# Rearranging the first two chunks of a fused retention and feed-forward kernel: load order, rounding order, matmuls of the identity, relative decays and another tail

## Chip, cores, metric

The kernel runs on one core of one Trainium2 chip. The metric is the device time of one execution in microseconds (us). A ratio of two kernels is the mean time of one kernel's fast runs over that of the other's of the same rounds, so it is not quite the ratio of the medians that are quoted beside it. Profiles show single executions: the profiled one of the kernel before took 1091.1 us, so a difference of two traces can be off by one or two us.

## The reference

```python
B, H, S, D = 8, 8, 576, 64                      # q, k, v: float32
scores = q @ k.transpose(0, 1, 3, 2) / sqrt(D)
gamma = 1 - 2.0 ** (-5 - arange(H))
ret = scores * where(i >= j, gamma ** (i - j), 0)   # per head
x = (ret @ v).transpose(0, 2, 1, 3).reshape(4608, 512)
h = x @ w_in                                    # 512 x 2048
g = h * erf(softplus(h))
out = g @ w_out                                 # 2048 x 512
```

## The kernel before

The retention is computed in 40 pieces of at most 128 tokens (five a batch, the fifth of 64). Each piece has three stages: `transposes` (q and k through TensorE, later q through VectorE), `scores` (TensorE, then a masked copy to `sT` on VectorE) and `outputs` (sT times v, q times the running state, the new k^T v, and the scaled result into the chunk's tile `x`). 512 tokens make a chunk. For each of nine chunks and each of four groups of hidden columns, a block `First` makes seven products of a Strassen-like scheme with w_in, and a block `Second` seven with w_out. I call the products by their operand: A11 is the first of a `First`, A12 its second, T2 the third of a `Second`. The prediction also writes T7, S7 and O7 for the three stages of piece 7; where it says T2 of chunk 0, it means the product.

Weights are rounded on the chip before use. A group has four parts of w_in and four of w_out; a part takes ScalarE, VectorE and GpSimd in turn, and the generator yields between steps, so that the program can place them:

```python
def rounding():
    while words:
        while words[0][2] > most_g[0]:
            yield
        ...
        nc.scalar.activation(a_f, high_f, AF.Abs)
        nc.scalar.mul(out=r_f, in_=low, mul=2.0**-52)
        yield
        nc.vector.tensor_scalar(out=a_f, in0=a_f, ..., op0=ALU.max, op1=ALU.min)
        yield
        nc.vector.tensor_scalar(out=a, in0=a, ..., op0=ALU.logical_shift_left, op1=ALU.bitwise_and)
        yield
        nc.vector.scalar_tensor_tensor(out=a, in0=high, ..., in1=a, ...)
        yield
        nc.vector.tensor_scalar(out=high, in0=a, ..., op0=ALU.bitwise_and)
        nc.gpsimd.tensor_tensor(out=r_f, in0=high_f, in1=r_f, op=ALU.mult)
        nc.gpsimd.tensor_tensor(out=a_f, in0=a_f, in1=r_f, op=ALU.add)
        load_weights()
        yield
        if sums:                       # last part of a group: four sums on VectorE
            yield from sums(*(w[:, i] for i in range(7)))
```

Every engine and the DMA-issuing SyncE take their instructions in order:

```python
load(0, "qkv"); ...constants...; load(1, "qkv"); load(2)    # load(2): k and v only
for _ in range(3):
    load_weights()
...
while done[0] < stages_for(TCH):          # pieces 0 to 3
    attend(done[0] + 1)
    if done[0] >= 2:
        round_weights(2)
operands_x(0, 0)                          # chunk 0's operands, and their store to DRAM
run(firsts[0].first(), (0, 1), 2)         # products, stages and rounding steps in turn
run(firsts[0].middle(), (0, 1, 2), 2)
run(firsts[0].last(), (0, 1), 2)
firsts[0].erf()
...
```

`operands_x` ends with `nc.sync.dma_start(out=xd[c], in_=t)`: groups 1 to 3 read the chunk's operands back from DRAM. The pool of `x` tiles has two buffers, so chunk 2's tile takes chunk 0's buffer and must wait for that store. In the tail, the last chunk's `multiply` (two products h * erf on VectorE) follows `last()` of the block before.

## Time and profile before

| | before |
|---|---|
| median of three runs | 1088.3 us (1087.9 to 1090.1) |
| span of the trace | 1089.4 us |
| TensorE busy | 1051.2 us |
| TensorE idle in the first 123.3 us | 29.3 us |
| TensorE idle in the last 29.4 us | 9.0 us |

Four moments divide the execution: the start of A11 of chunk 0 (42.3 us), of A11 of chunk 1 (88.1), of T2 of chunk 0 (123.3), and the start of the last product that is made in the same stretch in both kernels (1056.8). The line below is the stretch between the last two in the kernel before: length, then busy us and number of instructions for PE, PEld, DVE, ACT, POOL, then granted clock, DMA share and GB/s.

```profile
123.34:1056.80 933.46, 933.46 (x5480) 805.80 (x5477) 539.62 (x905) 349.63 (x430) 82.65 (x71) 1.00 0.49 165
1056.80:1089.40 32.60, 23.65 (x105) 19.24 (x103) 14.01 (x20) 7.16 (x7) 0.00 (x0) 1.00 0.17 66
```

The first line is TensorE without a gap at full clock. The second is the tail, 32.60 us, in which it idles 9.

### The profile page before, as it was taken

The page shows a single profiled execution, that of the slowest core. Times are in us where ns is not written, and L with a number is a line of the kernel's source. Part 1 is how long each engine was busy: PE and PEld are TensorE (multiplying, and loading weights), DVE is VectorE, ACT ScalarE, POOL GpSimd, SP SyncE. Part 2 cuts the span into 40 slices and gives each one's busy share as a digit, 9 for nine tenths or more (in the row PEclk, how much of TensorE's full clock was granted, in tenths as well). Part 3 has the DMA queues.
Part 4 walks back from the last instruction along what each step waited for, and adds up shares of the span by engine and source line. Part 5 has one row for each costly group of instructions (what it writes and reads, how often), then busy time and mean ns, then how long its engine had stood idle before and what let it go on. Part 6 is the DMA issues. An engine that isn't in the chain of part 4 may idle for free.

```text
span 1089.4 us, 15783 instructions
## 1 busy us (share of the span) xinstructions
PE 1051.2 (96%) x6472; PEld 901.3 (83%) x6472; DVE 625.4 (57%) x1074; ACT 397.2 (36%) x501; POOL 124.7 (11%) x110
## 2 busy tenths in 40 slices
PE   4899899999999999999999999999999999999996
PEld 3677788888888888888888888888888888888885
DVE  3738677577667663455555545555655445445444
ACT  2224322414324244433334444333344433333340
POOL 3313221121121000010001100110010000000000
PEclk8989899999999999999999999999999999999999
DMA  9787584665753253355555533555544333444432
GB/s 199 174 187 170 119 223 135 143 191 123 173 165 76 110 193 107 145 184 189 202 201 205 185 149 145 184 193 199 204 187 146 145 145 145 174 181 191 178 116 78
DMA packets 170376, 178.60 MB, mean 164 GB/s; under 512 B 144448, under 2 KB 144448, under 8 KB 162240
## 3 DMA queue, kind: packets, MB, share of 16 engines
q1 hardware_dynamic: 170160, 177.23, 51.5%
q8 instruction: 51, 0.84, 0.3%
q10 hardware_dynamic: 144, 0.36, 0.1%
q14 instruction: 21, 0.17, 0.1%
HBM read 123.30 MB, written 54.26 MB: 163 GB/s over the span
## 4 chain that ended last, share of the span: by engine, by line
PE 92%; DVE 3%; SPq 2%; DMA 2%; POOL 0%; issue 0%; DVEq 0%; POOLq 0%
PE a L511 23%; PE a L432 23%; PE g L511 12%; PE g L432 11%; PE e L432 6%; PE e L511 6%; PE o L323 3%; PE s L311 3%; PE o L334 3%; SPq L115 2%; PE kv L346 2%; PE pt_k L296 1%; DMA raw_q<-in_q_dram 1%; DVE t L92 1%; DMA wraw<-in_moe_w_in_dram 1%
## 5 line engine op out<-in xcount | busy, mean ns | idle before, releaser
L432 PE MATMUL a<-x,wa 128*128 128x256 f32 x1152 | 276.1, 383 | 0.0
L432 PEld LDWEIGHTS a<-x,wa 128*128 128x128 f32 x1152 | 217.4, 191 | 30.6 <-issue 0.4
L511 PE MATMUL a<-wb,s 128*128 128x256 f32 x864 | 205.9, 381 | 2.3 <-DVE o L92 2.3
L511 PEld LDWEIGHTS a<-wb,s 128*128 128x128 f32 x864 | 162.5, 190 | 26.1 <-DVE o L92 2.4
L92 DVE TENSOR_TENSOR t<-g,t 128x512 f32<-128x512 f32 x72 | 49.8, 691 | 159.6 <-ACT t L462 117.6
L432 PE MATMUL g<-x,wa 128*128 128x256 f32 x576 | 137.2, 381 | 0.0
L92 DVE TENSOR_TENSOR o<-a,o 128x512 f32<-128x512 f32 x108 | 74.3, 688 | 108.2 <-PE a L511 105.5
L432 PEld LDWEIGHTS g<-x,wa 128*128 128x128 f32 x576 | 108.2, 190 | 14.8
L236 POOL TENSOR_TENSOR wraw<-wraw 128x512 f32<-128x512 f32 x32 | 34.0, 1064 | 548.2 <-DVE wraw L235 312.6
L457 ACT COPY t<-a 128x512 f32<-128x512 f32 x36 | 21.1, 586 | 194.0 <-PE a L432 194.0
L92 DVE TENSOR_TENSOR t<-t,s 128x1024 f32<-128x1024 f32 x72 | 85.0, 1221 | 0.0
L474 ACT ACTIVATE s<-t 128x1024 f32<-128x1024 f32 x72 | 72.1, 1048 | 29.3 <-DVE t L92 29.3
L511 PE MATMUL e<-wb,t 128*128 128x256 f32 x288 | 69.7, 385 | 4.9 <-POOL wb L237 4.9
L468 ACT COPY t<-a 128x512 f32<-128x512 f32 x36 | 21.1, 586 | 143.1 <-PE a L432 143.1
L479 ACT ACTIVATE s<-s 128x1024 f32<-128x1024 f32 x72 | 72.1, 1049 | 0.4
L511 PE MATMUL a<-wb,t 128*128 128x256 f32 x288 | 68.6, 381 | 1.9 <-DVE t L92 1.9
L432 PE MATMUL e<-x,wa 128*128 128x256 f32 x288 | 70.2, 388 | 0.0
L511 PE MATMUL g<-wb,t 128*128 128x256 f32 x288 | 68.6, 381 | 0.0
L511 PE MATMUL g<-wb,s 128*128 128x256 f32 x288 | 68.5, 380 | 0.0
L276 POOL TENSOR_TENSOR raw_v<-raw_v,cst 128x512 f32<-128x512 f32 (+1 forms) x40 | 49.1, 1231 | 158.0 <-DMA raw_v<-in_v_dram 114.8
L511 PEld LDWEIGHTS e<-wb,t 128*128 128x128 f32 x288 | 54.6, 192 | 12.8 <-POOL wb L237 5.3
L511 PEld LDWEIGHTS a<-wb,t 128*128 128x128 f32 x288 | 54.1, 190 | 9.7 <-DVE t L92 2.3
(59 smaller groups left out, 1200.5 us busy)
## 6 DMA issues: line engine op xcount, KB each, us to landing
x<-xd SPq DMA_DIRECT2D x27, 1792.0 KB, 11.0
od<-o SPq DMA_DIRECT2D x54, 512.0 KB, 3.9
o<-od SPq DMA_DIRECT2D x27, 1024.0 KB, 7.3
xd<-x SPq DMA_DIRECT2D x9, 1792.0 KB, 6.5
out_dram<-o SPq DMA_DIRECT2D x18, 512.0 KB, 2.8
raw_k<-in_k_dram SPq DMA_DIRECT2D x64, 128.0 KB, 3.6
raw_v<-in_v_dram SPq DMA_DIRECT2D x64, 128.0 KB, 3.2
wraw<-in_moe_w_in_dram SPq DMA_DIRECT2D x32, 256.0 KB, 4.7
```

The source lines that it names most:

```text
L92: nc.vector.tensor_tensor(out=out, in0=in0, in1=in1, op=op)
L115: nc.sync.dma_start(out=t[:n, e::2, :], in_=heads.rearrange("h p d -> p h d"))
L236: nc.gpsimd.tensor_tensor(out=r_f, in0=high_f, in1=r_f, op=ALU.mult)
L276: nc.gpsimd.tensor_tensor(out=t[:n], in0=t[:n], in1=gk[:n, s0 // P, :].unsqueeze(2).to_broadcast([n, H, D]), op=ALU.mult,)
L311: nc.tensor.matmul(ps[e][:n, p, :n], lhsT=t["kT"][r, p, :n], rhs=t["qT"][r, p, :n], start=True, stop=True)
L323: nc.tensor.matmul(o[e * D : (e + 1) * D, p, :n], lhsT=t["v"][:n, 2 * p + e, :], rhs=t["sT"][:n, e, p, :n], start=(p == 0), stop=(s0 == 0 ...
L334: nc.tensor.matmul(o[r, p, :n], lhsT=kept["state"][r, p, :], rhs=t["qT"][r, p, :n], start=False, stop=(p == NP - 1), skip_group_check=True,)
L346: nc.tensor.matmul(kv[e * D : (e + 1) * D, p, :], lhsT=t["k"][:n, 2 * p + e, :], rhs=t["v"][:n, 2 * p + e, :], start=(p == 0), stop=(p == ...
L432: nc.tensor.matmul(acc[:, j * TH : (j + 1) * TH], lhsT=weights["wa", self.g][:, a, d, j * P : (j + 1) * P], rhs=x[self.g, self.c][a][:, d, :],
L474: nc.scalar.activation(self.s[:, j], t, AF.Softplus)
L479: nc.scalar.activation(self.s[:, j], self.s[:, j], AF.Erf)
L511: nc.tensor.matmul(acc[:, tp, :], lhsT=left[:, j * TH + tp * P : j * TH + (tp + 1) * P], rhs=weights["wb", self.g][:, b, j, :], start=(sta ...
```

## The change

Its intent: the inputs of all four pieces of chunk 0 come before any weights; the weights are rounded after piece 3; a stage of a further piece is emitted wherever TensorE might wait; matmuls of the identity keep its clock up before that. The decays become relative to the piece, so one table serves all pieces and the state takes one factor a piece on GpSimd. From batch 2 on, q is rearranged by a DMA from DRAM to DRAM and read back per piece. The store of chunk 0's operands moves behind its last product. The tail multiplies sooner and splits the last store.

```diff
-    load(0, "qkv")
+    load(0)                                    # q, k and v
...
-    load(1, "qkv")
-    load(2)
+    for i in range(1, 4):
+        load(i)
...
-            for p in range(NP):
-                nc.vector.scalar_tensor_tensor(out=x[0, c][:, p, at], ..., scalar=gs[:, j : j + 1], ...)
+            tt(x[0, c][:, :NP, at], o[:, :, a : a + m], gq[:, :, a : a + m], ALU.mult)
...
+                nc.gpsimd.tensor_tensor(out=new, in0=sums, in1=gp, op=ALU.mult)   # new state
...
-            nc.sync.dma_start(out=xd[c], in_=t)
+            x_stored[c] = t                    # store_x(c) issues it later
...
+    keep_busy(9)                               # matmuls of the identity
     weigh_values(0)
-    while done[0] < stages_for(TCH):
-        attend(done[0] + 1)
-        if done[0] >= 2:
-            round_weights(2)
+    for j in range(stages_for(TCH)):
+        attend(j + 1)
+        if j < 6:
+            keep_busy(2)
+        if j in (2, 5):
+            load_weights()
+            load_weights()
+    round_weights(5)                           # part 0
+    attend(done[0] + 2)
+    round_weights(5)                           # part 1
     operands_x(0, 0)
+    attend(done[0] + 3)
...
+    steps = firsts[0].first()
+    next(steps)                                # A11
+    round_weights(5)                           # part 2
+    attend(done[0] + 3)
+    round_weights(9)                           # part 3 and the sums
+    next(steps)                                # A12
+    attend(done[0] + 1)
+    run(firsts[0].middle(), (0, 2, 3))
+    run(firsts[0].last(), (3, 3))
+    store_x(0)
     firsts[0].erf()
...
             run(b.middle())
+            firsts[n + 1].multiply()
             run(b.last())
-            firsts[n + 1].multiply()
```

More of the change, by code (lines that the diff above doesn't have):

```diff
@@ L22 @@
 NP = H // 2
-NS = -(-S // P)
-CONST_COLS = NS * H + NP * P + NS * NP + P
+CONST_COLS = H + NP * P + NP + P
 HIGH_LEAST = float(np.array(0x38000000, np.uint32).view(np.float32))
@@ L37, in decays @@
     t = np.arange(P)
-    starts = np.arange(NS) * P
-    gk = pairs.T.reshape(1, 1, H) ** -(starts[None, :, None] + t[:, None, None])
+    gk = pairs.T.reshape(1, H) ** -t[:, None]
     row = pairs.repeat(D, axis=0)
     gq = row[:, :, None] ** t[None, None, :] / math.sqrt(D)
-    gs = row[:, None, :] ** starts[None, :, None]
+    gp = row**P
     tri = t[None, :] >= t[:, None]
-    return np.concatenate([x.reshape(P, -1) for x in (gk, gq, gs, tri)], axis=1).astype(np.float32)
+    return np.concatenate([x.reshape(P, -1) for x in (gk, gq, gp, tri)], axis=1).astype(np.float32)
 @with_exitstack
@@ L76 @@
     wpool = ctx.enter_context(tc.tile_pool(name="wpool", bufs=2))
-    wraw = ctx.enter_context(tc.tile_pool(name="wraw", bufs=3))
+    wraw = ctx.enter_context(tc.tile_pool(name="wraw", bufs=4))
     raw = ctx.enter_context(tc.tile_pool(name="raw", bufs=4))
@@ L98, with make_squares @@
     pieces = [(b, s0, min(P, S - s0)) for b in range(B) for s0 in range(0, S, P)]
-    loaded = {i: {} for i in range(len(pieces))}
+    loaded = {}
+    live = {}
     SQUARES = 2
     SQ = 32
-    def load(i, names="kv"):
-        if i >= len(pieces):
-            return
-        b, s0, n = pieces[i]
-        for name, src in (("q", q), ("k", k), ("v", v)):
-            if name in names and not (name == "q" and b >= SQUARES):
-                bufs = 2 if name == "q" else 4
-                t = raw.tile([P, H, D], FP32, tag=name, name=f"raw_{name}", bufs=bufs)
-                for e in range(2):
-                    heads = src[b, e * NP : (e + 1) * NP, s0 : s0 + n, :]
-                    nc.sync.dma_start(out=t[:n, e::2, :], in_=heads.rearrange("h p d -> p h d"))
-                loaded[i][name] = t
     squares = {}
-    def load_squares(b):
+    def make_squares(b):
         if SQUARES <= b < B:
-            t = squares[b] = raw.tile([P, NP, S // SQ, SQ], FP32, tag="q4", name="raw_q4", bufs=2)
+            t = squares[b] = dram.tile([P, NP, S // SQ, SQ], FP32, tag="sq", name="sq", bufs=B)
             for part in range(P // SQ):
@@ L128, in load_squares, with load @@
                 )
-    load(0, "qkv")
+    def load(i):
+        if i >= len(pieces) or i in loaded or i in live:
+            return
+        b, s0, n = pieces[i]
+        t = loaded[i] = {}
+        for name, src in (("q", q), ("k", k), ("v", v)):
+            t[name] = raw.tile([P, H, D], FP32, tag=name, name=f"raw_{name}", bufs=4)
+            if name == "q" and b >= SQUARES:
+                t[name] = t[name].rearrange("p h d -> p (h d)").rearrange("p (a i) -> p a i", a=NP)
+                nc.sync.dma_start(
+                    out=t[name][:, :, :n].rearrange("p a (s d) -> p a s d", d=SQ),
+                    in_=squares[b][:, :, s0 // SQ : (s0 + n) // SQ, :],
+                )
+                continue
+            for e in range(2):
+                heads = src[b, e * NP : (e + 1) * NP, s0 : s0 + n, :]
+                nc.sync.dma_start(out=t[name][:n, e::2, :], in_=heads.rearrange("h p d -> p h d"))
+    load(0)
     cst = cpool.tile([P, CONST_COLS], FP32, name="cst")
@@ L133 @@
     ends = [0]
-    for m in (NS * H, NP * P, NS * NP, P):
+    for m in (H, NP * P, NP, P):
         ends.append(ends[-1] + m)
-    gk, gq, gs, tri = (cst[:, a:b] for a, b in zip(ends, ends[1:]))
-    gk = gk.rearrange("p (s h) -> p s h", s=NS)
+    gk, gq, gp, tri = (cst[:, a:b] for a, b in zip(ends, ends[1:]))
     gq = gq.rearrange("p (a i) -> p a i", a=NP)
-    load(1, "qkv")
-    load(2)
+    gp = gp.unsqueeze(2).to_broadcast([P, NP, D])
+    for i in range(1, 4):
+        load(i)
     A11, S3, A12, A22, S1, S2, S4 = range(7)
@@ L203, in rounding @@
     def rounding():
-        while words:
-            while words[0][2] > most_g[0]:
+        while True:
+            while not words or words[0][2] > most_g[0]:
                 yield
@@ L241, in rounding @@
                 yield from sums(*(w[:, i] for i in range(7)))
-    for _ in range(3):
-        load_weights()
     round_step = rounding()
@@ L266, in x_tile @@
         return xpool.tile([P, n_dc + 3, TCH], FP32, tag="x", name="x")
-    live = {}
     kept = {}
+    weighed = set()
     def weigh_values(i):
-        if i < len(pieces):
-            _, s0, n = pieces[i]
-            t = loaded[i]["v"]
+        if i < len(pieces) and i not in weighed:
+            weighed.add(i)
+            n = pieces[i][2]
+            t = (loaded.get(i) or live[i])["v"]
             nc.gpsimd.tensor_tensor(
-                out=t[:n],
-                in0=t[:n],
-                in1=gk[:n, s0 // P, :].unsqueeze(2).to_broadcast([n, H, D]),
-                op=ALU.mult,
+                out=t[:n], in0=t[:n], in1=gk[:n, :].unsqueeze(2).to_broadcast([n, H, D]), op=ALU.mult
             )
@@ L286, in transposes @@
         load(i + 3)
-        load(i + 2, "q")
-        if s0 == 0:
-            load_squares(b + 1)
-        weigh_values(i + 1)
+        if s0 == P:
+            make_squares(b + 1)
+        if i < 8:
+            weigh_values(i + 1)
         for name in "qk":
             tT = t[name + "T"] = att.tile([P, NP, P], FP32, tag=name + "T", name=name + "T")
-            if name in t:
+            if name == "q" and b >= SQUARES:
+                nc.vector.transpose(out=tT[:, :, :n], in_=t[name][:, :, :n])
+            else:
                 pt = ps_at.tile([P, NP, P], FP32, tag="at", name=f"pt_{name}")
@@ L297, in transposes @@
                 nc.scalar.copy(out=tT[:, :, :n], in_=pt[:, :, :n])
-            else:
-                nc.vector.transpose(
-                    out=tT[:, :, :n].rearrange("p a (s i) -> p a s i", i=SQ),
-                    in_=squares[b][:, :, s0 // SQ : (s0 + n) // SQ, :],
-                )
     def scores(i):
@@ L353, in outputs @@
                     )
-            old = kept.get("state")
-            if pieces[i + 1][2] > D:
-                new = att.tile([P, NP, D], FP32, tag="state", name="state")
-                if s0 == 0:
-                    nc.scalar.copy(out=new, in_=kv)
-                else:
-                    tt(new, kv, old, ALU.add)
-            else:
+            half = pieces[i + 1][2] == D
+            sums = kv
+            if s0 > 0:
+                sums = att.tile([P, NP, D], FP32, tag="sums", name="sums")
+                tt(sums, kv, kept["state"], ALU.add)
+            if half:
                 new = states[b % 2]
                 for r in heads:
-                    tt(new[r, :, r], kv[r], old[r], ALU.add)
+                    nc.gpsimd.tensor_tensor(out=new[r, :, r], in0=sums[r], in1=gp[r], op=ALU.mult)
+            else:
+                new = att.tile([P, NP, D], FP32, tag="state", name="state")
+                (nc.gpsimd if s0 > 0 else nc.vector).tensor_tensor(out=new, in0=sums, in1=gp, op=ALU.mult)
             kept["state"] = new
+        weigh_values(i + 1)
         t0 = b * S + s0
@@ L373, in outputs @@
             at = slice(t0 - c * TCH, t0 - c * TCH + m)
-            for p in range(NP):
-                j = s0 // P * NP + p
-                nc.vector.scalar_tensor_tensor(
-                    out=x[0, c][:, p, at],
-                    in0=o[:, p, a : a + m],
-                    scalar=gs[:, j : j + 1],
-                    in1=gq[:, p, a : a + m],
-                    op0=ALU.mult,
-                    op1=ALU.mult,
-                )
+            tt(x[0, c][:, :NP, at], o[:, :, a : a + m], gq[:, :, a : a + m], ALU.mult)
             t0 += m
@@ L387 @@
     for i in range(len(pieces)):
-        if i + 1 < len(pieces):
-            stages.append((transposes, i + 1))
-        stages.append((outputs, i))
-        if i + 1 < len(pieces):
-            stages.append((scores, i + 1))
+        stages += [(transposes, i + 1), (outputs, i), (scores, i + 1)]
+        if i == TCH // P - 1:
+            stages[-3:-1] = stages[-2], stages[-3]
+    stages = [(of, i) for of, i in stages if i < len(pieces)]
     done = [0]
@@ L409, in load_x, with store_x @@
         nc.sync.dma_start(out=x[g, c], in_=xd[c])
+    def store_x(c):
+        nc.sync.dma_start(out=xd[c], in_=x_stored.pop(c))
+    x_stored = {}
     def operands_x(g, c):
@@ L500, in __init__ @@
             self.g, self.c = first.g, first.c
+            self.end = (self.g, self.c) == (n_g - 1, n_ch - 1)
         def begin(self):
@@ L558, in last @@
             self.store(0)
+            if self.end:
+                self.store(1, slice(OH, D_MODEL))
             yield
@@ L561, in last, with store @@
             self.add(1, 0, self.e)
-            self.store(1)
+            self.store(1, slice(0, OH if self.end else D_MODEL))
             yield
-        def store(self, half):
+        def store(self, half, os=slice(0, D_MODEL)):
             if self.g < n_g - 1:
-                nc.sync.dma_start(out=od[self.c][:, half], in_=self.o[:, half])
+                nc.sync.dma_start(out=od[self.c][:, half, :, os], in_=self.o[:, half, :, os])
             else:
@@ L570, in store @@
                 nc.sync.dma_start(
-                    out=out[r0 : r0 + TH, :].rearrange("(tp p) o -> p tp o", p=P), in_=self.o[:, half]
+                    out=out[r0 : r0 + TH, os].rearrange("(tp p) o -> p tp o", p=P), in_=self.o[:, half, :, os]
                 )
@@ L581, with keep_busy @@
         blocks += firsts[n + 1 : n + 2] + [seconds[n]]
-    weigh_values(0)
-    while done[0] < stages_for(TCH):
-        attend(done[0] + 1)
-        if done[0] >= 2:
-            round_weights(2)
+    idle = ps_e.tile([P, W], FP32, tag="g", name="idle")
+    def keep_busy(n):
+        for _ in range(n):
+            nc.tensor.matmul(idle[:, :P], lhsT=ident, rhs=ident, start=True, stop=True)
+    keep_busy(9)
+    weigh_values(0)
+    for j in range(stages_for(TCH)):
[8 more added lines that the diff above has]
+    round_weights(5)
     operands_x(0, 0)
+    attend(done[0] + 3)
     most = [stages_for(2 * TCH) - 1]
@@ L596, in run @@
             attend(min(done[0] + stages, most[0]))
-            if step in rounds:
-                round_weights()
-    run(firsts[0].first(), (0, 1), 2)
-    run(firsts[0].middle(), (0, 1, 2), 2)
-    run(firsts[0].last(), (0, 1), 2)
+            round_weights(rounds[step] if step < len(rounds) else 0)
+    steps = firsts[0].first()
[8 more added lines that the diff above has]
+    store_x(0)
     firsts[0].erf()
     most[0] = stages_for(3 * TCH) - 1
-    attend(stages_for(2 * TCH))
+    while done[0] < stages_for(2 * TCH):
+        attend(done[0] + 1)
+        round_weights(4)
     operands_x(0, 1)
-    round_weights(4)
-    run(firsts[1].first(), (0, 1))
+    store_x(1)
+    run(firsts[1].first(), (3, 3))
     firsts[0].multiply()
-    round_weights(4)
     for b, nxt in zip(blocks[1:], blocks[2:] + [None]):
@@ L617 @@
                 load_x(*order[n + 1])
-            run(b.middle(), (0, 1))
+            run(b.middle(), (1, 1))
             firsts[n - 1].sums()
-            if n == 1:
-                round_weights(9)
-            run(seconds[n - 1].first(), (0, 1))
+            run(seconds[n - 1].first(), (1, 1))
             run(b.last())
@@ L633 @@
             operands_x(*order[n + 2])
-            run(nxt.first(), (0,))
+            if n + 2 < n_ch:
+                store_x(n + 2)
+            run(nxt.first(), (1,))
             f.multiply()
-            run(b.last(), (1,))
+            run(b.last(), (0, 1))
         elif n + 1 < n_s:
```

## The prediction

> **What bounds the kernel now.** I read the page's busy row and slices first, then a table of the three head stages, the steady stage and the tail, then who PE waited for in the first 120 us, and last the timeline at those places and at the tail. Page (span, TensorE, granted clock):
>
> ```profile
> span 1089.4 us, 15783 instructions
> PE 1051.2 (96%) x6472; PEld 901.3 (83%) x6472; DVE 625.4 (57%) x1074; ACT 397.2 (36%) x501; POOL 124.7 (11%) x110
> ...
> PE   4899899999999999999999999999999999999996
> ...
> PEclk8989899999999999999999999999999999999999
> ```
>
> TensorE is the bound; only the first slices and the last one have room. The stage table (columns: window, its length, then busy us and instruction count of PE, PEld, DVE, ACT, POOL, granted clock, DMA share, GB/s) puts numbers on this:
>
> ```profile
> 0.00:5.20 5.20, 0.03 (x1) 0.06 (x1) 0.97 (x2) 1.28 (x1) 0.70 (x6) 1.00 0.70 165
> 5.20:42.30 37.10, 24.79 (x281) 20.48 (x281) 17.61 (x38) 10.10 (x19) 13.54 (x13) 0.86 0.99 194
> 42.30:88.10 45.80, 39.54 (x378) 31.91 (x376) 23.89 (x50) 14.96 (x24) 10.23 (x9) 0.89 0.75 175
> 88.10:123.30 35.20, 29.71 (x240) 23.86 (x236) 29.26 (x60) 14.03 (x22) 17.57 (x12) 0.90 0.75 175
> 123.30:380.00 256.70, 256.70 (x2345) 210.00 (x2342) 180.01 (x368) 80.31 (x115) 42.76 (x37) 1.00 0.55 146
> 380.00:1060.00 680.00, 680.00 (x3152) 598.63 (x3152) 360.56 (x538) 271.78 (x319) 39.89 (x34) 1.00 0.47 172
> 1060.00:1089.40 29.40, 20.45 (x90) 16.41 (x89) 13.06 (x18) 4.75 (x5) 0.00 (x0) 1.00 0.19 72
> ```
>
> The cuts at 42.3, 88.1 and 123.3 are where the first product of chunk 0, the first product of chunk 1 and the product T2 of chunk 0 start. From 123 to 1060 us PE is 100% busy at full clock: 3152 records in 680 us, 0.216 us each. Nothing can be won there without fewer matmuls. In the head it idles 5.2 + 12.3 + 6.3 + 5.5 = 29.3 us and the clock is short by 0.14 x 37.1 + 0.11 x 45.8 + 0.10 x 35.2 = 13.7 us; as PE is busy some 80% of the time, that is about 11 us of work. In the tail it idles 9 us. So at most 44 us (4%) is there, less the 5 us before the first input lands and 4 us after the last product.
>
> Who PE waited for up to 120 us (us in total, times, longest):
>
> ```profile
> PE pt_q L296 <- DMA raw_q<-in_q_dram: 11.3, 3, 5.2
> PE s L311 <- ACT kT L297: 6.4, 2, 5.7
> PE e L511 <- POOL wb L237: 4.9, 1, 4.9
> PE o L323 <- DVE sT L92: 2.2, 4, 1.0
> ```
>
> The 5.7 us wait for kT (13.2 to 19.0 us) is not the copy's fault: ScalarE sits in program order behind the rounding of the first weights, which land at 16.7. Then q of piece 2, issued behind them, lands at 25.0 (4 us), and q of piece 5 costs 2.2 us at 75.8. The last is 4.9 us at 107 to 112, for w_out weights not rounded yet.
>
> **What the skill says.** (1) "TensorE: Matmul & The Clock Gate", Part 1: the clock is halved by default and released after a busy window of about 3.4 us, lost after an idle one. The trace agrees: 16 score records take 2.08 us at 8.2 and 19.0 us, after waits, and 1.16 at 30.2. (2) "SBUF — State Buffer", Who interferes with whom: a VectorE instruction with two SBUF inputs or in a 2-port mode and a GpSimd one lock each other out. The trace agrees: the scaling of v takes 1.04 us alone and 4.19 at 97.5, amid VectorE work. (3) "DMA: Bandwidth & Descriptors", Specifications: below 512 B a DMA engine does read-modify-write. The trace before has 144448 such packets, but not the DRAM-to-DRAM form that is added; no row shows its cost.
>
> **The change, part by part.**
>
> *Load order and the first four pieces.* Before, pieces 0 to 2 and three weight parts (0.5 MB each) are loaded, piece 3 behind them. After, all of pieces 0 to 3 come first: 3.07 MB plus 0.33 MB of constants. The first 20 us moved 4.1 MB, some 0.23 MB/us once started at 2.5, so piece 2 is there at 14, piece 3 at 17.5, weight parts 0 and 1 at 21.5 and 24 (with half piece 4 before them), 2 and 3 at 29.5 and 32. Nothing of rounding stands before piece 3 in ScalarE's order. One piece then cycles in: scores 1.1 + masked copy to sT 1.4 + outputs 0.95 + state part 1.03 + kv 0.6 = 5.1 us at full clock (the transposes, 0.9, fit into the 1.4). From scores at 7.7: 4.1 + 3 x 5.1 gives 27, plus about 1 for 21 matmuls of the identity in the way: outputs of piece 3 end at **28.5**, against 42.2 before.
>
> *Rounding of chunk 0's weights.* Now behind that. A part needs ScalarE 1.3, VectorE 1.85 (0.42 + 0.42 + 0.69 + 0.42), GpSimd 2.3 (1.04 + 1.28). GpSimd also scales v (1.04), and most of these lock each other out: 1.85 + 2.3 + 1.04 = 5.2 us a part. Two parts from 30 on: first product of chunk 0 at **40** (42.3 before, but now with four more stages, about 5 us of work, done). Without any locking out, parts 2 and 3 give the second product (A12) at 46.5; with full locking 52.5. I take **49** (48.7 before), PE idling about 3 before 40 and 4 before 49.
>
> *From there to chunk 1.* Left are A12, five products (1.9 each with switching), T7, O6, S7, T8, O7, S8, T9, O8: 11.4 + about 13 = 25 us, plus 1 of cold clock: first product of chunk 1 at **75**, not 88.1. That is 13 us.
>
> *w_out weights.* 25 rounding steps are called between A12 and the end of chunk 1's first products; they need 24. So the 4.9 us wait at 107 goes, and with it the cold stretch behind it (clock 0.66 at 110 to 120, about 2 us). Minus a new wait of under 1 us: 6 to 7 us.
>
> *Relative decays.* Four VectorE operations (1.12 us) become one (about 0.69), at some 36 pieces; the states' factor goes to GpSimd (about 0.5 each). In the head this shortens PE's wait for a free PSUM buffer (0.7 us in all); later VectorE is 70% busy and off the path: nothing.
>
> *q through DRAM.* From batch 2 on, q is rearranged into DRAM and read back per piece: 256 KB more a piece, 7.5 MB in all, plus writes of 128 B. DMA share at 123 to 380 is 0.55; an estimate of 0.7 after, loads three pieces (25 us) ahead: hidden.
>
> *Tail.* The product of sums g*erf goes ahead of the last step: PE's 1.9 us wait at 1068.4 goes (VectorE does the two, 2.35 us, from 1065.3), and 0.5 of the next wait. The last store is 256 KB instead of 512, whose transfer took some 1.6 us: 0.7. Sum 3.
>
> **Sum:** 13 + 7 + 3 = 23, less 1 for new small waits: 1088.3 - 22 = **1066 us**.
>
> **Rivals.** (a) *VectorE and GpSimd become the head's bound.* Rounding now falls into a denser stretch; VectorE was 98% busy at 90 to 110 already. If locking is full and PE goes cold at 44 to 52, the first product of chunk 1 comes at 81 to 82: 1072. For it: the 4.19 us above. Against it: at 50 us the two engines took turns, 1.45 us for a 1.04 us scaling. (b) *PE is kept fed throughout*: A12 at 46, no cold stretch, chunk 1 at 72, no later waits: 1059. For it: data is in place early enough by the sums above, and the step counts look fitted. (c) *DMA gives it back*: SyncE issues in order, and a load of q must wait for the DRAM copy; if 128 B writes cost double, waits appear at 120 to 380 as PE waits for raw_q or weights: 1070 to 1080. Against it: share 0.55 and the distance of three pieces. (d) *Only the waits move*: total as before. Against: 12 us of waits in the first 30 us have a cause that is removed.
>
> **Range and chances.** Rival (b) sets the low end, (a) with some of (c) the high one: 1057 to 1075. The 2% line is at 1067, a microsecond from my number. I lean to the lower side a little, since the stages look fitted: faster 0.52, within 2% 0.46, slower 0.02.
>
> **What would show it.** Outputs of piece 3 end near 28.5 us; first product of chunk 0 near 40; A12 near 49 after a wait of several us for GpSimd; chunk 1 near 75; T2 near 103; no wait for w_out weights; PE 100% from there on, with DMA share near 0.7; tail 3 us shorter. I am wrong if A12 comes after 54, if PE waits reappear after 120 us, or if the clock stays low after 50.

## The result, and the profile after

The changed kernel took 1086.0 us (median of four, 1085.2 to 1086.2) against 1089.2 (four runs): ratio 0.9969, 95% interval 0.9951 to 0.9986. That is 0.3% faster, within 2%, and outside the range that was predicted. A second measurement in other rounds (label e0_after) gave 0.9969 again.

Page of the changed kernel: span, busy row, slices of TensorE and of its granted clock.

```profile
span 1083.4 us, 15779 instructions
PE 1053.2 (97%) x6514; PEld 904.8 (84%) x6514; DVE 611.5 (56%) x942; ACT 395.2 (36%) x494; POOL 143.6 (13%) x142
...
PE   9596999999999999999999999999999999999997
...
PEclk9898999999999999999999999999999999999999
```

The first slice (27 us) has gone from 4 tenths busy to 9, but the second stands at 5 and the fourth at 6, where the kernel before had 8 and 9. The clock is still low in the second and fourth. The same stretches as before, cut at the same four moments:

```profile
5.30:36.30 31.00, 28.25 (x370) 24.16 (x368) 14.79 (x25) 8.51 (x16) 10.79 (x12) 1.00 1.04 195
36.30:80.65 44.35, 33.64 (x314) 27.18 (x313) 29.11 (x45) 15.56 (x24) 16.68 (x16) 0.88 0.85 182
80.65:119.99 39.34, 30.51 (x241) 24.42 (x237) 26.41 (x45) 13.77 (x21) 12.55 (x12) 0.87 0.77 207
119.99:1053.45 933.46, 933.46 (x5481) 805.80 (x5478) 526.43 (x808) 348.88 (x427) 102.89 (x98) 1.00 0.52 172
1053.45:1083.40 29.95, 23.38 (x105) 19.32 (x103) 13.82 (x20) 7.16 (x7) 0.00 (x0) 0.98 0.20 71
```

The long stretch has the same length to a hundredth of a us, 933.46, although VectorE has 97 instructions fewer in it and the DMA share rose from 0.49 to 0.52: relative decays and q through DRAM neither helped nor hurt there. The tail is 29.95 against 32.60. And the head is 120.0 against 123.3: its first stretch is shorter (36.3 against 42.3), the second about the same (44.4 against 45.9), the third *longer* (39.3 against 35.2).

What TensorE waited for in the first 120 us of the changed kernel (us in total, times, longest):

```profile
PE e L426 <- POOL wa L240: 6.3, 2, 4.5
PE a L426 <- DVE x L90: 6.1, 1, 6.1
PE a L426 <- POOL wa L240: 4.0, 1, 4.0
PE s L308 <- ACT kT L299: 2.4, 2, 2.1
```

Gone are the waits for q behind the start (6.1 us of 11.3; during the other 5.2, the first load, identities run now), the 5.7 us for kT of piece 1 and the 4.9 for rounded w_out weights: 16.7 us. In their place stand 10.3 us for rounded w_in weights (the rows with `wa`) and 6.1 us for `x`. The next two fences show where these come from. First VectorE, GpSimd, ScalarE and TensorE between 33 and 55 us, chosen lines (start, length, engine and line, what it writes and reads, then idle time before it):

```profile
34.46 1.40 DVE L229 TENSOR_SCALAR wa<-wa 128x512 uint32<-128x512 uint32 x1
...
35.89 1.41 DVE L233 SCALAR_TENSOR_TENSOR wa<-wraw,wa 128x512 uint32<-128x512 uint32 x1
...
37.68 5.26 DVE L90 TENSOR_TENSOR x<-x 128x512 f32<-128x512 f32 x4
...
39.34 1.60 POOL L240 TENSOR_TENSOR wa<-wa,wraw 128x512 f32<-128x512 f32 x1
...
44.11 0.67 ACT L220 ACTIVATE wa<-wraw 128x512 f32<-128x512 f32 x1
...
48.94 0.79 DVE L225 TENSOR_SCALAR wa<-wa 128x512 f32<-128x512 f32 x1
...
49.49 0.70 PE L426 MATMUL e<-x,wa 128*128 128x256 f32 x2 [1.80 <-POOL wa L240]
...
53.34 1.28 POOL L240 TENSOR_TENSOR wa<-wa,wraw 128x512 f32<-128x512 f32 x1
...
54.67 2.93 PE L426 MATMUL e<-x,wa 128*128 128x256 f32 x6 [4.48 <-POOL wa L240]
```

Operations that took 0.43 and 0.69 us elsewhere take 1.4 here, and four that took 2.6 (in a quiet place) take 5.3, while GpSimd works beside them. The third part does not start on ScalarE before 44.1, behind the copy of A11's result, and the fourth not on VectorE before 48.9, behind piece 6. So A12's last weights are ready at 54.6: two of its eight matmuls run at 49.5, the other six at 54.7.

Then SyncE's queue, VectorE and TensorE around the 6.1 us wait:

```profile
75.77 6.98 SPq L203 DMA_DIRECT2D wraw<-in_moe_w_in_dram  x4
82.80 0.59 SPq L401 DMA_DIRECT2D xd<-x  x1
...
85.39 3.47 PE L426 MATMUL e<-x,wa 128*128 128x256 f32 x8
...
88.64 0.86 PE L298 MATMUL pt_k<-ident,raw_k 128*128 128x128 f32 x4
...
92.17 0.42 DVE L90 TENSOR_TENSOR x<-o,cst 128x256 f32<-128x256 f32 x1 [8.01 <-DMA xd<-x]
...
95.58 3.75 PE L426 MATMUL a<-x,wa 128*128 128x256 f32 x8 [6.08 <-DVE x L90]
```

VectorE stands for 8 us in front of the first write into chunk 2's `x`, because the buffer still holds chunk 0's operands and their store, `xd<-x`, was issued at 82.8 us only. The program asks for that store behind chunk 0's last product, which ended at 75.5; another 7 us went by in SyncE's own order, where four weight loads (75.77 to 82.75) stood before the store and waited 4.5 us for their buffers. The store then took 9.3 us to land. Everything behind it in VectorE's order waits too, among it chunk 1's operands. The two products around the gap run at about half speed, 3.47 and 3.75 us where 1.99 is usual (the granted clock was 0.50 from 86 to 89 us).

### The profile page after: what moved, and what is told of

The parts are those of the page before. It is cut to its first block, busy times and chain, and to the rows that moved or that the text cites. A ratio compares the mean times of both kernels' runs of the same rounds, so it can differ in the third digit from the quotient of the medians.

```text
span 1083.4 us, 15779 instructions
## 1 busy us (share of the span) xinstructions
PE 1053.2 (97%) x6514; PEld 904.8 (84%) x6514; DVE 611.5 (56%) x942; ACT 395.2 (36%) x494; POOL 143.6 (13%) x142
## 4 chain that ended last, share of the span: by engine, by line
PE 93%; DVE 3%; DMA 1%; POOL 1%; issue 1%; ACT 1%; SPq 0%; POOLq 0%; DVEq 0%
PE a L506 23%; PE a L426 23%; PE g L506 12%; PE g L426 11%; PE e L426 6%; PE e L506 6%; PE s L308 3%; PE o L320 3%; PE o L331 3%; PE kv L343 2%; PE pt_k L298 1%; DMA xd<-x 1%; PE idle L585 1%; DVE x L90 0%; DVE sT L90 0%
## 5 line engine op out<-in xcount | busy, mean ns | idle before, releaser
L451 ACT COPY t<-a 128x512 f32<-128x512 f32 x36 | 21.1, 586 | 193.0 <-PE a L426 193.0
L462 ACT COPY t<-a 128x512 f32<-128x512 f32 x36 | 21.1, 586 | 146.7 <-PE a L426 146.7
L426 PEld LDWEIGHTS e<-x,wa 128*128 128x128 f32 x288 | 55.6, 196 | 14.9 <-POOL wa L240 6.9
L456 ACT COPY t<-a 128x512 f32<-128x512 f32 x36 | 21.1, 585 | 113.4 <-PE a L426 113.4
L90 DVE TENSOR_TENSOR sT<-s,cst 128x512 f32<-128x512 f32 (+1 forms) x80 | 47.0, 629 | 26.8 <-PE s L308 26.7
```

The source lines that it names most:

```text
L90: nc.vector.tensor_tensor(out=out, in0=in0, in1=in1, op=op)
L426: nc.tensor.matmul(acc[:, j * TH : (j + 1) * TH], lhsT=weights["wa", self.g][:, a, d, j * P : (j + 1) * P], rhs=x[self.g, self.c][a][:, d, :],
L451: nc.scalar.copy(out=self.t1[:, 1], in_=self.a)
L456: nc.scalar.copy(out=self.t2[:, 1], in_=self.a)
```

## Experiments

Every ratio is to the kernel before, in the same rounds.

| run | median us | ratio (95% interval) | A12 can go on at | A11 of chunk 1 | T2 of chunk 0 |
|---|---|---|---|---|---|
| before (first trace) | 1089.2 | 1 | 48.7 | 88.1 | 123.3 |
| changed (e0_after) | 1085.3 | 0.9969 (0.9956 to 0.9981) | 54.9 | 80.5 | 119.8 |
| e3_before_tail | 1085.7 | 0.9968 (0.9954 to 0.9981) | 49.6 | 86.8 | 122.0 |
| e11_before_decays | 1089.9 | 1.0004 (0.9989 to 1.0018) | 47.5 | 89.4 | 124.4 |
| e4_no_identity | 1087.2 | 0.9976 (0.9964 to 0.9988) | 55.5 | 82.6 | 122.7 |
| e1_store_early | 1081.8 | 0.9925 (0.9912 to 0.9938) | 54.8 | 80.7 | 116.5 |
| e5_dve_round | 1085.6 | 0.9960 (0.9947 to 0.9974) | 53.6 | 79.2 | 118.3 |
| e6_round_sooner | 1082.2 | 0.9940 (0.9927 to 0.9952) | 51.6 | 79.0 | 117.1 |
| e7_sooner_early | 1078.7 | 0.9906 (0.9891 to 0.9921) | 50.0 | 77.4 | 111.5 |
| e8_sooner_early_wb | 1078.2 | 0.9898 (0.9885 to 0.9912) | 50.5 | 80.0 | 113.6 |
| e9_best | 1074.4 | 0.9866 (0.9847 to 0.9885) | 48.8 | 78.3 | 109.1 |
| e10_best_dve | 1074.0 | 0.9855 (0.9839 to 0.9871) | 49.0 | 78.0 | 108.9 |
| e12_final | 1072.1 | 0.9840 (0.9826 to 0.9853) | 45.9 | 75.4 | 106.3 |

All twelve gave correct results. The moments come from one trace each. The head of e3_before_tail is that of the kernel before, and still A11 of chunk 1 and T2 of chunk 0 come 1.3 us sooner in it and A12 0.9 us later, so a difference of a us or so between two moments shows little. My theory after reading the result was: the head's early gain is given back in two places, the late store and the rounding order. The rivals were: DMA is short from 40 us on, and VectorE and GpSimd simply have too much to do.

### The changed kernel again

> The changed kernel itself, for a comparison in the same rounds as the three below. Theory (the tail gives nearly all of the gain, the head nothing to 2 us): ratio to before 0.995 to 0.998.

As expected: 0.9969. Its waits are those of the first trace: 4.0 us in A11, 4.5 in A12, 6.1 for `x`.

### The tail alone, on the kernel before

The edit is the tail part of the change, alone: `multiply` before `last()`, and the last store in two halves.

> The kernel before with the change's tail alone (products of the last chunk ahead of the last step, last store halved). Theory: 2.7 us of the gain is the tail, as the two traces differ by 2.7 us from the T2 of chunk 0 to the end: 1086.0 to 1087.0 us against 1089.2. Rival (the tail is worth nothing, the head gave all 3 us): 1089 us.

Ratio 0.9968: the tail alone gives as much as the whole change. Everything else together is worth nothing that these runs resolve; the intervals, some 0.0013 to either side each, leave room for some 2 us either way. The traces say the same from the other side: T2 of chunk 0 starts at 122.0 us in this run, whose head is that of the kernel before, and at 119.8 and 120.0 in the changed one.

### The relative decays alone, on the kernel before

```diff
-            for p in range(NP):
-                nc.vector.scalar_tensor_tensor(...)
+            tt(x[0, c][:, :NP, at], o[:, :, a : a + m], gq[:, :, a : a + m], ALU.mult)
...
+                nc.gpsimd.tensor_tensor(out=new, in0=sums, in1=gp, op=ALU.mult)
```

For want of memory the sum is kept in the state's tile here, not in one of its own.

> The kernel before with the relative decays alone (smaller tables, one VectorE product per piece in place of four, the state's factor on GpSimd). Theory (VectorE is off the path after the head, and in the head nothing waits for these for more than 0.7 us): within 2 us of the kernel before, 1087 to 1090 us. Rival (the state's detour over GpSimd puts a new wait into the state products): 1090 to 1093 us.

Ratio 1.0004: worth nothing by itself, as the theory said.

### The changed kernel without the matmuls of the identity

```diff
-    keep_busy(9)
...
-        if j < 6:
-            keep_busy(2)
```

> The changed kernel without the 21 matmuls of the identity. Theory A (they keep the clock up in the first four pieces): the scores of the first pieces take 2.08 us instead of 1.16, outputs of piece 3 end 2 to 4 us later than 29.4 us, and the time is 1088 to 1090 us. Theory B (they only fill gaps, the weights' rounding is what chunk 0 waits for): first products at the same times, 1085 to 1087 us.

Theory A missed in size. Only the scores of piece 0 take 2.08 us; those of piece 1 take 1.16 already. The outputs of piece 3 end 0.5 us later (k^T v of piece 3 starts at 29.24 instead of 28.74). The chunk's products come 0.5 to 2.7 us later by this one trace, the time ratio is 0.9976 against 0.9969, and their intervals overlap. So the identities were worth half a us at the place they were put for, by one trace; whether 0.7 us of time is real stays open.

### The early store, on the changed kernel

```diff
-            x_stored[c] = t
+            if c == 0:
+                nc.sync.dma_start(out=xd[c], in_=t)
+            else:
+                x_stored[c] = t
...
-    store_x(0)
```

> The changed kernel with one move: chunk 0's operands are stored to DRAM as soon as they are made, as before the change, instead of after its last product. Theory (the late store holds the x buffer, so VectorE waits 8.0 us at 84 to 92 us, TensorE 6.1 us behind it, and the clock drops): that wait is gone, T2 of chunk 0 starts 7 to 10 us before 120.0 us, time 1077 to 1079 us. Rival (the stretch from 40 us on is short of DMA, so the early 1.8 MB only delays weights and pieces): the wait moves to pieces or to w_out weights, time within 2 us of the changed kernel, 1084 to 1088 us.

VectorE's wait for the buffer is gone, and TensorE's for `x` is 0.9 us. What VectorE waited for at 80 to 110 us is now this:

```profile
DVE wb L90 <- POOL wb L240: 2.4, 1, 2.4
DVE wb L225 <- ACT wb L220: 2.2, 2, 1.3
```

A12's weights and A11 of chunk 1 come at the same times as in the changed kernel (54.8 and 80.7 us), so the early 1.8 MB delayed nothing, and the rival of the short DMA falls for this store. T2 starts 3.5 us sooner and the ratio drops by 0.0044, some 4.8 us. The theory's cause is right; its 7 to 10 us were too many, for the stretch still has a 2.1 us wait for kT, one of 2.6 us for the transposed q behind w_out's sums on VectorE, and a product at about half speed after each.

### GpSimd's part of the first weights on VectorE, on the changed kernel

```diff
-            nc.gpsimd.tensor_tensor(out=r_f, in0=high_f, in1=r_f, op=ALU.mult)
-            nc.gpsimd.tensor_tensor(out=a_f, in0=a_f, in1=r_f, op=ALU.add)
+            eng = nc.vector if (name, g) == ("wa", 0) else nc.gpsimd
+            eng.tensor_tensor(out=r_f, in0=high_f, in1=r_f, op=ALU.mult)
+            eng.tensor_tensor(out=a_f, in0=a_f, in1=r_f, op=ALU.add)
```

> The changed kernel with the last multiply and add of the first four weight parts on VectorE instead of GpSimd. Theory (VectorE and GpSimd lock each other out at 33 to 55 us and so stretch the rounding): a part takes 3.3 us on VectorE without stretching, the second product of chunk 0 gets its last weights at 48 to 50 us instead of 54.6, chunk 1 starts 4 to 6 us earlier than 80.7, but the wait for the x buffer stays or grows by as much, since the store's issue hangs on SyncE's waits: 1081 to 1086 us. Rival (VectorE's own work is the bound of that stretch): A12 comes at 54 us or later, 1086 to 1088 us.

A miss for the theory: A12 can go on at 53.6 us, only a us sooner. The locking out is gone (chunk 0's four operand operations take 2.61 us instead of 5.26), but VectorE now works without a break from 29.5 to 43.1 us, stands for 1.1 us until ScalarE hands it the third part, and works on to 53.5. The lock is real, but taking it away did not make A12 early: nearly the same lateness comes from one in-order engine that gets all four parts after piece 3. The edit also gives VectorE some 5.5 us more to do (eight operations of 0.69), so it does not price the lock alone.

### The rounding begun sooner, on the changed kernel

```diff
-        if j in (2, 5):
+        if j in (0, 5):
             load_weights()
             load_weights()
+        if j == 10:
+            round_weights(5)          # part 0, ahead of the outputs of piece 3
     round_weights(5)                  # part 1
-    attend(done[0] + 2)
-    round_weights(5)
-    operands_x(0, 0)
-    attend(done[0] + 3)
+    attend(done[0] + 5)
+    round_weights(10)                 # parts 2 and 3, ahead of A11
+    operands_x(0, 0)
...
-    next(steps)
-    round_weights(5)
-    attend(done[0] + 3)
-    round_weights(9)
+    next(steps)
+    attend(done[0] + 3)
+    round_weights(4)                  # the sums
     next(steps)
```

> The changed kernel with one thing moved: the rounding of chunk 0's first weights is no longer strung out behind piece 3. Two weight parts are loaded before piece 4, the first part is rounded before the outputs of piece 3 in program order, the third and fourth before chunk 0's first product. Theory (the order of the in-order queues, not VectorE's total work, makes A12 late): first product without the 4 us wait at 36 us, A12's last weights at 44 to 47 us instead of 54.6, chunk 1's first product 7 to 10 us before 80.7 us; but the wait for the x buffer then grows or stays, as the store is still late, so 1078 to 1084 us. Rival (VectorE and GpSimd have too much to do from 29 us on, whatever the order): A12 at 52 us or later, 1084 to 1088 us.

In between. A12 goes on at 51.6, not at 44 to 47, and A11 of chunk 1 comes 1.6 us sooner, not 7 to 10; the time, 1082.2, lies in the range given (it is 3.1 us under the changed kernel). A12 still waits 2.6 us for its weights, and TensorE waits for `x` about as long as before (6.6 us). There is also a new wait: the outputs of piece 3 wait 2.1 us for the state on GpSimd (`PE o L331 <- POOL state L362`). That is the relative decays' new step, and it queues behind the scaling of piece 4's v, whose load now comes behind two weight parts. The edit moves the loads of the first two parts together with their rounding; how much each is worth was not tested apart.

### Both of these

The edits of e1_store_early and e6_round_sooner together.

> The one before plus the early store of chunk 0's operands. If the two losses are separate they add: 7 to 10 us and 4 to 5 us off the changed kernel, 1071 to 1076 us. Rival (either one merely hides behind the other): no more than 2 us better than the better of the two alone, 1078 to 1082 us.

1078.7 us: 0.0063 below the changed kernel's 0.9969, where the store alone gave 0.0044 and the order alone 0.0029, 0.0073 in sum. So they are separate losses that add within the intervals. The total lies above the 1071 to 1076 written down, since the order gained less than I had given it.

### The error function later, w_out sooner

```diff
-    run(firsts[0].middle(), (0, 2, 3))
-    run(firsts[0].last(), (3, 3))
-    firsts[0].erf()
+    run(firsts[0].middle(), (4, 4, 4))
+    run(firsts[0].last(), (4, 4))
     ...
     while done[0] < stages_for(2 * TCH):
         attend(done[0] + 1)
+        if done[0] == stages_for(2 * TCH) - 1:
+            firsts[0].erf()
         round_weights(4)
```

> The one before, with the error function of chunk 0 put after the transposes' copies of the next piece on ScalarE, and the w_out weights rounded a few steps sooner. Theory (the 2.1 us wait for kT and the 2.6 us wait for qT behind the weights' sums, with the cold clock they bring, are worth 3 to 6 us): 1067 to 1072 us. Rival (rounding sooner crowds VectorE in the stretch of chunk 0's products): 1072 to 1078 us.

Inconclusive in time: 0.9898 against 0.9906. The 2.1 us wait for kT is gone, the state's wait is 2.1 us in this trace (1.0 in that of e7), and the one for chunk 1's operands has grown from 2.6 to 4.0 us: w_out was rounded so soon that the next group's weights were worked on next, and ScalarE stood 2.9 us in front of one of these that had not landed (`ACT wa L220 ... <-DMA wraw<-in_moe_w_in_dram`).

### The version built from these

Two weight parts are loaded before piece 4 and both rounded before piece 3's outputs, part 2 before the outputs of piece 4, part 3 before A11; piece 4's v is scaled behind the state's factor; the store is early; no rounding stands between the transposes of piece 9 and chunk 1's operands except the last w_out sums. The diff is against the changed kernel.

```diff
-        if j in (2, 5):
+        if j in (0, 5):
             load_weights()
             load_weights()
-    round_weights(5)
-    attend(done[0] + 2)
-    round_weights(5)
-    operands_x(0, 0)
-    attend(done[0] + 3)
+        if j == 10:
+            round_weights(10)
+    attend(done[0] + 3)
+    round_weights(5)
+    attend(done[0] + 2)
+    round_weights(5)
+    operands_x(0, 0)
...
-        if i < 8:
+        if i < 8 and i != 3:
             weigh_values(i + 1)
...
+        if done[0] == stages_for(2 * TCH) - 1:
+            firsts[0].erf()
+            round_weights(4)
-        round_weights(4)
```

The rest (early store, rounding steps in `middle` and `last`) is as in the run before.

> The version built from what was found: two weight parts before piece 4 and both rounded before the outputs of piece 3, the third before the outputs of piece 4, the fourth before chunk 0's first product; the scaling of v of piece 4 behind the state's factor on GpSimd (in the kernel before this one the state waited 2.1 us behind it); early store; error function later; no weights of the next group rounded while chunk 1's operands are made. Theory (queue order is what is left): A12's last weights at 44 to 47 us, T2 of chunk 0 at 105 to 109 us, 1070 to 1075 us. Rival (VectorE and GpSimd are simply full from 26 to 52 us): A12 at 50 us again, 1076 to 1079 us.

1074.4 us, inside the theory's range. TensorE does not wait in A12 at all any more; T2 starts at 109.1 us. It now waits 3.4 us at the outputs of piece 4 for its v, which stands behind two parts on GpSimd.

Next, the edit of e5 for the third and fourth part alone, on top of this:

```diff
+            eng = nc.vector if (name, g, slot) == ("wa", 0, A12) else nc.gpsimd
```

> The one before with the multiply and add of the third and fourth weight part on VectorE instead of GpSimd. Theory (locking out costs more than the 2.8 us of VectorE work): A12 1 to 3 us sooner than there, 1069 to 1074 us. Rival (VectorE is the one that is full): A12 the same or later, the time the same or up to 2 us more.

A12 comes at 49.0 instead of 48.8, not sooner, and 0.9855 against 0.9866 is not told apart. The theory's 1 to 3 us did not come: which engine does these two steps made no difference that shows here, once the order was changed.

The last edit, on top of that one:

```diff
         if j == 10:
-            round_weights(10)
+            weigh_values(4)           # v of piece 4 ahead of the parts
+            round_weights(5)
+    round_weights(5)
```

> The last one with the scaling of v of piece 4 back ahead of the rounding on GpSimd (the outputs of piece 4 waited 3.5 us for it there), and the second weight part rounded behind the outputs of piece 3. Theory (queue order on GpSimd): outputs of piece 4 start at 33 to 35 us instead of 37.5, chunk 0's first product at 38 to 40 us instead of 42.5, no cold clock there, 1070 to 1072 us. Rival (the weights then come later by as much): 1073 to 1076 us.

1072.1 us, 1.6% faster than the kernel before (0.9840) and 1.3% faster than the changed one by the two ratios, 0.9840 / 0.9969. The outputs of piece 4 start at 34.5 us, A11 at 39.4, A12 runs without a wait at 45.9, T2 at 106.3 us. Chunk 0's first product still runs slowly (3.19 us against 1.99), so that part of the expectation missed; the outputs of piece 4 still wait 2.4 us, for sT. Its stretches, cut at the same moments:

```profile
5.30:39.35 34.05, 29.32 (x369) 24.98 (x368) 19.83 (x31) 11.18 (x20) 14.45 (x14) 0.94 1.04 199
39.35:75.41 36.06, 32.97 (x315) 26.46 (x313) 29.56 (x51) 15.14 (x25) 12.28 (x11) 0.92 0.96 225
75.41:106.30 30.89, 28.53 (x241) 22.95 (x237) 26.14 (x41) 11.95 (x17) 14.07 (x11) 0.94 1.02 237
106.30:1039.76 933.46, 933.46 (x5480) 805.80 (x5477) 522.67 (x803) 347.90 (x425) 101.48 (x96) 1.00 0.53 172
```

The long stretch is 933.46 us once more, in spite of the DMA share of 0.53. Against the changed kernel the first stretch is 3.1 us longer and the second 8.3 shorter, since the rounding that A11 waited for there now comes before it: 5.2 us net. The third is 8.5 us shorter. These are the places of the two losses that were named.

## Why the prediction was wrong

**The bound, and where there is room: right.** TensorE is the bound, nothing can be won between T2 of chunk 0 and the tail (933.46 us in all three kernels cut here), and what can be won lies in the head and the tail. The "at most 44 us" of room is a slip, as its terms give 29.3 + 11 + 9 = 49; nothing was built on it.

**First four pieces: right.** Outputs of piece 3 were to end at 28.5 us; they ended at 29.4 (k^T v at 28.74 plus 0.69). That is 13 us sooner than before. Its 1 us for the identity's matmuls "in the way" had the wrong sign: without them these outputs end 0.5 us later (e4). The loads were later than its sums: ScalarE got the first weight part at 27.0 us, not 21.5, as SyncE issued it from 20.5 on only. Nothing hung on that here, since VectorE did not come to that part before 30.5.

**Rounding of chunk 0's weights: the term that failed first.** A11 at 40 was right (its weights were complete at 41.0). For A12 the prediction said "Without any locking out, parts 2 and 3 give the second product (A12) at 46.5; with full locking 52.5. I take 49". It was 49.5 for two matmuls and 54.7 for the other six, above the range that the step itself had set. The lock was seen: "SBUF — State Buffer", Who interferes with whom, says that VectorE with two SBUF inputs or in a 2-port mode and GpSimd block each other for whole instructions, and the trace agrees (5.26 us instead of 2.61 for four operations). What was missed is that the parts do not queue behind each other but behind other work in program order: part 2 behind A11's copy on ScalarE (44.1 us), part 3 behind piece 6 on VectorE (48.9). Without GpSimd in it A12 still came at 53.6 (e5); with parts, and the first two loads, moved in the order, at 51.6, 48.8 and 45.9 (e6, e9, e12). That the parts queue behind other work is seen on ScalarE: it idled 10.6 us until A11's result could be copied at 43.6, although the third part had landed by 38.3 (issued by 31.7, at most 6.6 us to land). Rival (a) has its share in this: VectorE was busy 9.8 and 9.5 of the 10 us from 30 and from 40 us on. But from 20 to 30 us it was busy 4.2 us only, and that is where the new order puts the first of this work.

**From there to chunk 1: right.** "25 us, plus 1 of cold clock" after A12: 80.65 - 54.67 = 26.0. Only the start was late, so A11 of chunk 1 came at 80.65 and not at 75. That is 5.7 of the 17 us by which T2 of chunk 0 missed its 103 us. Rival (a) had named 81 to 82 for it.

**From chunk 1 to T2: the largest miss, 11.3 of the 17 us.** The prediction saw a gain here: "the 4.9 us wait at 107 goes, ... Minus a new wait of under 1 us: 6 to 7 us". The old wait did go. But the stretch, 35.2 us before, was to be 28 and became 39.3. The listed waits in it are 2.1 + 6.1 + 0.6 = 8.8 us, and two products at about half speed add 1.5 + 1.8 = 3.2 us; with 27.3 us of work (the 30.51 us that TensorE is busy in it, less these 3.2) that makes 39.3. The work was foreseen: before, it was 29.7 us busy, less some 2.3 us of low clock. The change part by part never mentions that the store of chunk 0's operands was moved, although the diff shows it; a buffer that is freed by a store is a wait that moves with the store. e1, which moves nothing but the store, shows this loss to be worth 0.0044 of the time, some 4.8 us. Even then the stretch is 35.8 us long: its waits for kT (2.1), for the transposed q (2.6) and for `x` (0.9) and its two slow products (3.1 in all) were not in the prediction either. "TensorE: Matmul & The Clock Gate", Part 1, has the clock halved again after an idle window; here a product ran at half speed behind an idle gap of only 2.1 us (3.47 us at 85.4), which the sum had not counted.

**Tail: right.** 3 us predicted; 2.65 by the two traces (32.60 - 29.95), and the tail alone gave 0.9968, some 3.5 us.

**Relative decays and q through DRAM: right in time.** "Nothing" for the first (e11: 1.0004), "hidden" for the second, which no run tried alone: no wait in the long stretch, with a DMA share of 0.66 at 120 to 380 us, where 0.7 was estimated and 0.55 stood before. One thing was overlooked, the state's new dependence on GpSimd, which made no wait in the changed kernel and one of 1.0 to 2.1 us as soon as the loads were moved (e6 to e8). The copy's added reads came to 7.1 MB, not 7.5.

**Sum.** 13 + 7 + 3 - 1 = 22 was written; 7.5 - 4.1 + 2.7 = 6.1 came by the first two traces, and 3.4 by time (0.0031 of 1089), as the first trace of the kernel before was a slow one of its kind. What the head as a whole brought is not resolved: about 0 by time, with room for some 2 us either way, and 2.0 to 3.3 us by the traces' T2. The chances were drawn from the fact that "the stages look fitted", which was no measurement; 1071 to 1075 us could be had with this structure, as e9 to e12 show, but not with this order.

## What to carry to other kernels

When inputs are fetched sooner, write down for each in-order queue (every engine, and the engine that issues DMAs) what now stands in front of what, not only how much each engine has to do: the change removed 16.7 us of waits and let as much back in through the order of rounding (10.3) and the late store (6.1). A store that frees a buffer belongs next to its last producer, or at least early enough to land before the next writer arrives; moved "out of the way", and behind loads that themselves waited, it became an 8 us wait of VectorE. And measure small parts of a large change alone: here the tail's few lines carried the whole gain, as far as the runs resolve it.

## What the Trainium skill lacked or had wrong

- "SBUF — State Buffer", Who interferes with whom: it says that whoever issues first gets the shared ports for a whole instruction, not who comes next when both have a queue. Here they took turns, one instruction each: between 37.7 and 42.9 us four VectorE operations took 0.68, 1.41, 1.76 and 1.52 us (2.61 for all four in a quiet place), the three GpSimd operations beside them 1.36, 1.60 and 1.47 us instead of 1.04 to 1.28, and their ends alternate (38.4, 39.3, 39.8, 40.9, 41.5, 42.4, 42.9). That fits whole-instruction locks, if the time an instruction stands waiting counts in its length.
- "TensorE: Matmul & The Clock Gate", Why this matters for your kernels: the advice is no idle gap above about 3 us. A gap of 2.1 us before the second product of chunk 1 was followed by a product at about half speed in the changed kernel and in e1 (3.47 and 3.56 us), and by one at full speed in e6 and e7 (1.99 us both). So a gap below 3 us was not always safe, and its length alone did not decide.
- "DMA: Bandwidth & Descriptors", Specifications: no figure for a copy from DRAM to DRAM in runs of 128 B. The 24 such DMAs of 288 KB took a median of 5.2 us to land; the form before, into SBUF, had 4.7.
